# Weights in smaller transfers, masks moved to TensorE and a later order of work in a sparse-attention and feed-forward kernel

## The chip, the cores and the metric

The kernel runs on one core of a Trainium2 chip. The metric is device time in microseconds (us). Before the change it is 330.48 us, the median of three runs (329.52 to 330.79). One execution of each kernel was also profiled; the profile's span is some 2 us shorter than the device time.

The core has five engines that run side by side, each through its own instructions in the order of the program: TensorE (PE in the profile; its weight loads are PEld), VectorE (DVE), ScalarE (ACT), GpSimd (POOL) and SyncE (SP). Here TensorE writes its results to eight banks of the memory called PSUM, which ScalarE and VectorE empty. Loads run on 16 shared DMA engines.

## The reference

```python
scores = scale * np.matmul(q, k.transpose(0, 1, 3, 2))          # 8 batches, 8 heads, 576 positions, 64 wide
mask_local = (rel >= 0) & (rel < 32)                            # heads 0 to 3
mask_strided = (rel >= 0) & (pos[None] % 32 == pos[:, None] % 32)   # heads 4 to 7
attn = softmax(np.where(masks, scores, -1e9)); x = attn @ v
# ... x to (4608 tokens, 512)
h = x @ w_in                       # 512 -> 2048
g = s * np.maximum(h, 0)**2 + b
out = g @ w_out                    # 2048 -> 512
```

## The kernel before

Attention goes batch by batch, in four pairs of heads: Q and K are transposed (TensorE, or a DMA transpose for the strided K of batches 2 to 7), scores go to a PSUM bank, ScalarE takes the exponential, and the product with V follows. The feed-forward runs over nine blocks of 512 tokens: 64 matmuls of 512 columns for `x @ w_in`, ScalarE's relu, VectorE's square, 64 matmuls for `g @ w_out`.

A host-side plan decides the order in which all this is issued. It keeps assumed times: when a load lands, how long an instruction takes. Each engine then gets its instructions in that order. An assumed landing that is wrong makes an engine stand still at the head of its queue, as e1 below shows; the reads wait for their semaphores.

```python
LAT = {"A": 70.0, "V": 70.0, "P": 70.0, "D": 2000.0}      # assumed latency, ns; D is a DMA transpose
...
def load_w_in():
    wv = moe_w_in.rearrange("(c p) f -> p c f", p=128)
    for c, (at, n) in enumerate(((0, 512), (512, 512), (1024, 1024))):
        nc.gpsimd.dma_start(out=w_in_sb[c], in_=wv[:, :, at:at + n])
...
# scores; only batch 0 gets its mask as a matmul (identity times -30000 where masked)
if b == 0:
    nc.tensor.matmul(out=st["s", g][0:nk, c:c + 2 * nq], lhsT=ident[0:nk, 0:nk],
                     rhs=neg_loc if loc else neg_str, start=True, stop=False)
nc.tensor.matmul(out=st["s", g][0:nk, c:c + 2 * nq], lhsT=..., rhs=..., start=b > 0, stop=True)
# the other batches: VectorE multiplies the exponentials by a mask of 0 and 1
nc.vector.tensor_tensor(out=pt[0:nk, 0:2 * n], in0=pt[0:nk, 0:2 * n], in1=mask, op=ALU.mult)
...
by_dma = b >= 2          # strided K, and X of the local pairs, by DMA transpose from batch 2 on
...
def landing(cost):       # assumed landing of the next load in the queue
    nonlocal ring
    ring = max(ring, plan.t + 2000.0) + cost
    return ring
```

While nothing is ready in the first microseconds, the plan issues filler matmuls on a tile of ones (L792 in the profile before) to keep TensorE's clock up.

The softmax here doesn't subtract the row's maximum and nothing guards it: scores larger than these inputs give would overflow.

## Time and profile before

| | before |
|---|---|
| device time, median of 3 | 330.48 us |
| span of the profiled execution | 328.9 us |
| TensorE busy | 319.1 us, 97% |
| VectorE, ScalarE busy | 201.4, 168.8 us |
| granted TensorE clock, mean (1 is full speed) | 0.992 |

A busy time counts a matmul from its start to its modelled end, and matmuls overlap (those of 512 columns last some 380 ns and start 216 ns apart). So this document works with starts. The **needed** time of TensorE is the number of matmuls of each shape by the usual distance from start to next start; the **lost** time is what the actual distances have beyond it (a wait, or half clock, at which 512 columns take 427 ns); the **filler** time is that of the filler matmuls. First start, needed, lost and filler add up to the end of the last matmul by their definition: before, 1.07 + 303.8 + 10.5 + 9.4 = 324.8 us, and the trace has 324.74. All three are worked out from TensorE's timeline; the prediction shows the distances.

### The profile page before, as it was taken

How to read it: one execution, taken by the hardware profiler on the slowest of the kernel's cores; microseconds unless marked ns; L12 is line 12 of the kernel's file. 1: busy time of each engine (PE TensorE's matmuls, PEld its weight loads, DVE VectorE, ACT ScalarE, POOL GpSimd, SP SyncE). 2: the span in 40 equal slices, each digit the busy share in tenths (PEclk: the TensorE clock that was granted, in tenths of full speed). 3: DMA queues.
4: the chain of work that ended last, by engine and by line, in shares of the span. 5: the costliest groups of instructions: out<-in, count | busy, mean ns of one | idle time of the engine just before them, and what ended most of it. 6: DMA issues, size and time to landing. Idle time of an engine off the chain costs nothing.

```text
span 328.9 us, 6347 instructions
## 1 busy us (share of the span) xinstructions
PE 319.1 (97%) x2407; PEld 182.0 (55%) x2407; DVE 201.4 (61%) x553; ACT 168.8 (51%) x319; POOL 82.2 (25%) x112
## 2 busy tenths in 40 slices
PE   8969999999999999999999999999999999999994
PEld 3755655666556666556656556655444544444442
DVE  5665866689877867876777878786332432333211
ACT  2755954499727987754664445553532433233100
POOL 7361549746126434412710000000000000000000
PEclk9998999999999999999999999999999999999999
DMA  8999999999999999949994320111001000100021
GB/s 119 172 177 205 214 154 171 210 170 158 137 146 147 135 58 182 134 64 101 148 117 55 81 84 2 51 52 64 2 32 64 32 34 33 64 31 35 32 98 64
DMA packets 74472, 33.13 MB, mean 101 GB/s; under 512 B 55882, under 2 KB 68810, under 8 KB 74442
## 3 DMA queue, kind: packets, MB, share of 16 engines
q0 software_dynamic: 49984, 18.65, 55.0%
q1 hardware_dynamic: 24458, 14.07, 21.1%
q8 instruction: 19, 0.31, 0.4%
q14 instruction: 11, 0.09, 0.1%
HBM read 38.15 MB, written 9.44 MB: 145 GB/s over the span
## 4 chain that ended last, share of the span: by engine, by line
PE 89%; DMA 6%; DVE 2%; ACT 1%; issue 1%; SPq 0%; POOL 0%; POOLq 0%; DVEq 0%
PE ps_f L601 38%; PE ps_f L566 36%; PE ps_s L421 4%; PE ps_a L473 4%; PE ps_t L350 3%; DMA w_in_sb<-in_moe_w_in_dram 3%; DMA w_out_sb<-in_v_dram 2%; PE ps_t L521 2%; DMA ql<-in_q_dram 1%; PE ps_a L624 1%; PE ps_s L566 1%; ACT u L584 1%; ACT qD_loc L280 1%; DVE qD_str L280 1%; PE ps_f L473 0%
## 5 line engine op out<-in xcount | busy, mean ns | idle before, releaser
L566 PE MATMUL ps_f<-xT,w_in_sb 128*128 128x512 f16 x568 | 154.0, 381 | 0.0
L601 PE MATMUL ps_f<-w_out_sb,gT 128*128 128x512 f16 x576 | 151.8, 379 | 0.4 <-DVE gT L590 0.4
L584 ACT ACTIVATE u<-ps_f 128x512 f16<-128x512 f32 x138 | 82.0, 597 | 83.3 <-PE ps_f L566 61.1
L590 DVE TENSOR_TENSOR gT<-u 128x512 f16<-128x512 f16 x144 | 59.4, 420 | 55.3 <-ACT u L584 54.6
L566 PEld LDWEIGHTS <-w_in_sb 128*128 128x128 f16 x576 | 61.7, 114 | 43.9 <-DMA w_in_sb<-in_moe_w_in_dram 2.1
L601 PEld LDWEIGHTS <-gT 128*128 128x128 f16 x576 | 54.2, 98 | 50.4 <-DVE gT L590 1.1
L435 ACT ACTIVATE pt<-ps_s 128x384 f16<-128x384 f32 (+2 forms) x96 | 44.8, 488 | 15.7 <-PE ps_s L421 15.1
L473 PEld LDWEIGHTS <-pt 72*72 72x72 f16 (+1 forms) x448 | 35.2, 119 | 13.2 <-DVE x_nat L499 0.2
L612 DVE SCALAR_TENSOR_TENSOR o<-ps_f,s_sb,bcs 128x512 f32<-128x512 f32 x36 | 26.8, 745 | 20.6 <-PE ps_f L601 20.3
L499 DVE TENSOR_TENSOR x_nat<-ps_a,rec 72x256 f16<-72x256 f32 (+1 forms) x76 | 35.0, 461 | 1.7
L488 DVE RECIPROCAL rec<-ps_a 72x4 f32<-72x4 f32 (+1 forms) x76 | 13.7, 181 | 18.5 <-PE ps_a L473 16.3
L258 POOL DMA_DIRECT2D v_loc<-in_v_dram x28 | 24.3, 875 | 1.7 <-issue 0.9
L263 POOL DMA_DIRECT2D v_str<-in_v_dram x16 | 13.5, 844 | 44.5 <-PE ps_a L473 22.8
L473 PE MATMUL ps_a<-v_str,pt 72*72 72x65 f16 x204 | 20.9, 196 | 0.0
L421 PE MATMUL ps_s<-qD_str,kTs 128*72 128x144 f16 x128 | 20.1, 226 | 0.2 <-ACT kTs L280 0.2
L280 ACT COPY xT<-ps_t 128x576 f16<-128x576 f16 x16 | 10.2, 637 | 14.1 <-PE ps_t L521 14.0
L421 PEld LDWEIGHTS <-kTs 128*72 128x72 f16 x128 | 13.0, 113 | 5.7 <-ACT kTs L280 0.4
L473 PE MATMUL ps_a<-v_loc,pt 128*96 128x65 f16 x150 | 16.2, 203 | 0.0
L421 PE MATMUL ps_s<-qD_loc,kT_loc 128*128 128x192 f16 x96 | 16.0, 246 | 0.0
L443 DVE TENSOR_TENSOR pt<-pt,mask_str 72x432 f16<-72x432 f16 (+1 forms) x42 | 14.3, 349 | 2.8 <-ACT pt L435 2.5
L443 DVE TENSOR_TENSOR pt<-pt,mask_loc 128x384 f16<-128x384 f16 x42 | 14.2, 351 | 2.2 <-ACT pt L435 1.8
L521 PEld LDWEIGHTS <-x_nat 72*128 72x128 f16 (+1 forms) x152 | 9.9, 102 | 6.5 <-DVE x_nat L499 1.1
(87 smaller groups left out, 253.6 us busy)
## 6 DMA issues: line engine op xcount, KB each, us to landing
out_dram<-o SPq DMA_DIRECT2D x36, 256.0 KB, 2.0
ql<-in_q_dram POOLq DMA_DIRECT2D x8, 288.0 KB, 6.6
kl<-in_k_dram POOLq DMA_DIRECT2D x8, 288.0 KB, 7.5
v_loc<-in_v_dram POOLq DMA_DIRECT2D x28, 80.0 KB, 11.4
w_out_sb<-in_moe_w_out_dram POOLq DMA_DIRECT2D x4, 512.0 KB, 12.0
qs<-in_q_dram POOLq DMA_DIRECT2D x6, 288.0 KB, 8.6
ks<-in_k_dram POOLq DMA_DIRECT2D x6, 288.0 KB, 9.5
v_str<-in_v_dram POOLq DMA_DIRECT2D x16, 72.0 KB, 4.6
```

The lines of the kernel that those rows point to most:

```text
L258: nc.gpsimd.dma_start(out=vl[:, h, 1:LT, 0:D], in_=rest[:, h])
L280: {"A": nc.scalar.copy, "V": nc.vector.tensor_copy, "P": nc.gpsimd.tensor_copy}[eng](**kw)
L421: nc.tensor.matmul(out=st["s", g][0:nk, c:c + 2 * nq], lhsT=(st["k"][:, i * nq:i * nq + nk] if loc else st["k"][:, i, 0:SQ]), rhs=st["q"][ ...
L435: nc.scalar.activation(out=pt[0:nk, 0:2 * n].rearrange("k t c -> k (t c)"), in_=st["s", g][0:nk, 0:2 * n * nq], func=AF.Exp, scale=scale)
L443: nc.vector.tensor_tensor(out=pt[0:nk, 0:2 * n], in0=pt[0:nk, 0:2 * n], in1=mask, op=ALU.mult)
L473: nc.tensor.matmul(out=st["a"][0:nq, j % per, :], lhsT=st["pt", g][0:nk, i, :], rhs=vt[0:nk, 2 * mm + e, j, :])
L499: nc.vector.tensor_tensor(out=st["x"][:, j0:j0 + per, 64 * e:64 * e + 64], in0=st["pa", e, j][0:nq, 0:per, 0:D], in1=st["rec", e, j][0:nq, ...
L566: nc.tensor.matmul(out=gts["h", T, ft], lhsT=w_in_sb[min(ft // 4, 2)][:, ct, :].rearrange("p (c x l) -> p c l x", x=128, l=4)[:, max(ft // ...
L584: nc.scalar.activation(out=gts["u", T, ft], in_=gts["h", T, ft], func=AF.Relu)
L590: nc.vector.tensor_tensor(out=gts[T][:, ft, :], in0=u, in1=u, op=ALU.mult)
L601: nc.tensor.matmul(out=gts["o", T, ts], lhsT=gts[T][:, ft, ts * 128:(ts + 1) * 128], rhs=w_out_sb[:, ft, :], start=(ft == 0), stop=(ft == ...
L612: nc.vector.scalar_tensor_tensor(out=o, in0=gts["o", T, ts], scalar=s_sb[:, 0:1], in1=bcs, op0=ALU.mult, op1=ALU.add)
```

## The change

The intent: use w_in's first quarter as its pieces arrive, relieve VectorE by giving the masks of batches 1 and 2 to TensorE, take K of batch 2 off the DMA queue, and place work on later loads later, where it will not be waited for. The core of the diff, cut:

```diff
-    LAT = {"A": 70.0, "V": 70.0, "P": 70.0, "D": 2000.0}
+    LAT = {"A": 70.0, "V": 70.0, "P": 70.0, "D": 5000.0}
...
+            for c in FIRST:                       # FIRST = (2, 0, 1, 3), the order of use
+                nc.gpsimd.dma_start(out=w_in0[c], in_=wv[:, c, 0:512])
+        else:                                     # issued later, after V of batch 0 is cast
+            nc.gpsimd.dma_start(out=w_in_sb[0], in_=wv[:, :, 512:1024])
+            nc.gpsimd.dma_start(out=w_in_sb[1], in_=wv[:, :, 1024:2048])
...
-        by_dma = b >= 2
+        k_by_dma, x_by_dma = b >= 3, b >= 2
...
-                if b == 0:
+                if b < PE_MASK:                   # PE_MASK = 3
...
-        return ring
+        return ring + (6000.0 if plan.t > 60000.0 else 0.0)
...
     def fetch_qk(b):
+        for mm in range(2):                       # wait until K of the batch before has landed
+            if (b - 1, "kTs", mm) in loaded:
+                nc.gpsimd.tensor_copy(out=gate[0:1, 2 + mm:3 + mm],
+                                      in_=loaded[b - 1, "kTs", mm][0:1, 0, 0:1])
```

Four parts, then: **four transfers** (with the later issue of the weights after them), **masks**, **K of batch 2**, and **placing**.

More of the change, by code (lines that the diff above doesn't have):

```diff
@@ L129 @@
     PS = 512
+    FIRST = (2, 0, 1, 3)
     NFT = DFF // 128
@@ L170 @@
     b_sb = const.tile([128, 1], FP32)
-    w_in_sb = [const.tile([128, 4, n], FP16, name=f"w_in_sb{i}")
-               for i, n in enumerate((512, 512, 1024))]
+    w_in0 = [const.tile([128, 512], FP16, name=f"w_in0{i}") for i in range(4)]
+    w_in_sb = [const.tile([128, 4, n], FP16, name=f"w_in_sb{i}") for i, n in ((1, 512), (2, 1024))]
     w_out_sb = const.tile([128, NFT, DM], FP16)
@@ L265, in load_vs, with load_w_in @@
                 in_=v[b, 4 + h].rearrange("(p j) d -> p j d", j=ST))
-    def load_w_in():
+    def load_w_in(first):
         wv = moe_w_in.rearrange("(c p) f -> p c f", p=128)
-        for c, (at, n) in enumerate(((0, 512), (512, 512), (1024, 1024))):
-            nc.gpsimd.dma_start(out=w_in_sb[c], in_=wv[:, :, at:at + n])
+        if first:
+            for c in FIRST:
[3 more added lines that the diff above has]
+            nc.gpsimd.dma_start(out=w_in_sb[1], in_=wv[:, :, 1024:2048])
     def load_w_out(chunks):
@@ L310 @@
     TB, SB, AB, F1B, F2B = 1, 2, 1, 2, 2
+    PE_MASK = 3
     ps = {tag: [psum.tile([128, PS], FP32, name=f"ps_{tag}{i}") for i in range(n)]
@@ L392, in k_dma @@
             nc.sync.dma_start_transpose(out=st["k"], in_=ks[b % 2][:, 1024 * mm:1024 * mm + 1024])
-        if by_dma and not loc:
+            loaded[b, "kTs", mm] = st["k"]
+        if k_by_dma and not loc:
             plan.post([("in", "ks", b, mm), ("s", (b - 1, m), 2)], {"D": 1000.0}, k_dma,
@@ L398, in pair_steps @@
         for name in ("q", "k"):
-            if by_dma and not loc and name == "k":
+            if k_by_dma and not loc and name == "k":
                 continue
@@ L422, in f @@
                     out=st["s", g][0:nk, c:c + 2 * nq], lhsT=(st["k"][:, i * nq:i * nq + nk] if loc else st["k"][:, i, 0:SQ]),
-                    rhs=st["q"][:, i].rearrange("d e c -> d (e c)"), start=b > 0, stop=True)
-            s = Step(f, (2 if b == 0 else 1) * (2 * nq / 2.4 + 8), needs=[("q", id_), ("k", id_)],
+                    rhs=st["q"][:, i].rearrange("d e c -> d (e c)"), start=b >= PE_MASK, stop=True)
+            s = Step(f, (2 if b < PE_MASK else 1) * (2 * nq / 2.4 + 8), needs=[("q", id_), ("k", id_)],
                      group=group if i % per_s == 0 else None)
@@ L448, in score @@
                             [("p", id_, g)])]
-                if b == 0:
+                if b < PE_MASK:
                     s.posts = [([key], {"A": 170 + 0.83 * 2 * n * nq}, ex, [("p", id_, g), group])]
@@ L545, in x_dma @@
                 in_=st["x"].rearrange("p t d -> p (t d)"))
-        if by_dma and loc:
+        if x_by_dma and loc:
             plan.post([("x", id_, e, nt - 1) for e in range(2)], {"D": 1000.0}, x_dma,
@@ L566, in f @@
             nc.tensor.matmul(
-                out=gts["h", T, ft], lhsT=w_in_sb[min(ft // 4, 2)][:, ct, :].rearrange(
+                out=gts["h", T, ft], lhsT=(w_in_sb[min(ft // 4, 2) - 1][:, ct, :] if ft > 3 else w_in0[ct]).rearrange(
                     "p (c x l) -> p c l x", x=128, l=4)[:, max(ft // 4 - 2, 0), ft % 4],
@@ L572, in ff1 @@
                  for c in ((ct,) if early else range(4))]
-        needs.append(("w_in", ft // 4))
+        needs.append(("w_in", ft // 4) if ft > 3 else ("w_in0", ct))
         if ft == 0 and ct == cts[0] and T >= 2:
@@ L702, in weights_in, with more_weights @@
         nc.gpsimd.tensor_copy(out=gate[0:64, 2:4].bitcast(FP32), in_=vl_stage[64:128, 0, 0, 0:1])
-        load_w_in()
-        ring = 17700.0
-        for keys, cost in ([0], 2900), ([1], 2900), ([2, 3], 5000):
+        load_w_in(True)
+        ring = 18000.0
+        for c in FIRST:
+            arrive([("w_in0", c)], landing(650))
+    def more_weights(eng):
+        load_w_in(False)
+        for keys, cost in ([1], 2800), ([2, 3], 5700):
             arrive([("w_in", c) for c in keys], landing(cost))
     plan.done[("first",)] = 13700.0
-    plan.post([("first",)], {"P": 3500.0}, weights_in, [("w",)])
+    plan.post([("first",)], {"P": 2800.0}, weights_in, [("w1",)])
+    plan.post([("w1",)] + both("vl", 0), {"P": 1500.0}, more_weights, [("w",)])
     plan.done["raw", "v", True, 0] = 16200.0
@@ L747 @@
                     [("fetch_v", b + 1) if b else ("free",)] +
-                    [("k", (b, mk)) for mk in range(4)], {"P": 0.0},
+                    [("k", (bk, mk)) for bk in (b, b + 1 if b > 1 else b) for mk in range(2, 4)],
+                    {"P": 0.0},
                     lambda eng: fetch_qk(b + 2), [("fetch", b + 2)]))
@@ L758 @@
             gr = [Group(*x) for x in (("s", SB), ("s", SB), ("f1", F1B), ("f1", F1B))]
-            cts = (2, 0, 1, 3)
+            cts = FIRST
             f1 += [ff1(T, ft, ct, gr[ft], cts, True) for ct in cts for ft in range(4)]
```

## The prediction

> **What bounds the kernel now.** I read the page first, then the busy time by stretch of 10 us, then TensorE's timeline from 6 to 46 us with GpSimd's beside it, then the list of waits.
>
> ```profile
> PE 319.1 (97%) x2407; PEld 182.0 (55%) x2407; DVE 201.4 (61%) x553; ACT 168.8 (51%) x319; POOL 82.2 (25%) x112
> PE 89%; DMA 6%; DVE 2%; ACT 1%; issue 1%; SPq 0%; POOL 0%; POOLq 0%; DVEq 0%
> ```
>
> And of the groups with every shape kept apart (busy us, mean ns of one | idle before):
>
> ```profile
> L418 PE MATMUL ps_s<-neg_str,ident 72*72 72x144 f16 x16 | 2.7, 227 | 0.1
> L418 PE MATMUL ps_s<-neg_loc,ident 128*128 128x192 f16 x12 | 2.5, 245 | 0.0
> L443 DVE TENSOR_TENSOR pt<-pt,mask_loc 128x384 f16<-128x384 f16 x42 | 14.2, 351 | 2.2 <-ACT pt L435 1.8
> ```
>
> TensorE is the bound: 97% busy, and 89% of the chain that ended last. So time falls only if TensorE is given less work or waits less. The mean durations (227 ns) are latencies; what a matmul costs is the distance from its start to the next start. From the timeline: 512 columns 216 ns (24 of them in 5.34 us), a local score or mask (192 columns) 82 ns, a strided one (144 columns) 63 to 65 ns, a transpose 42 ns (96 columns) or 32 ns (72), a product with V 34 ns. With the counts of the groups: 1168 x 0.216 = 252.3; scores 96 x 0.082 + 128 x 0.063 = 15.9; masks of batch 0 12 x 0.082 + 16 x 0.065 = 2.0; transposes of Q and K 192 x 0.042 + 160 x 0.032 = 13.2; products with V 448 x 0.034 = 15.2; transposes of X 128 x 0.032 + 24 x 0.043 = 5.1. Together 303.7 us of needed work. Of the span of 328.9, 6.9 go before the first useful matmul and 4.2 after the last one, so some 14 are lost between, to waits, to half clock and to the filler matmuls of L792. Adding up, from the timeline, what each start-to-start distance has over the usual one gives where: about 5 before 20 us (3.5 of it filler while the first inputs land), 4.4 from 20 to 30, 0.9 from 30 to 40, 2.9 from 40 to 110, 1.6 from 110 to 230, nothing after.
>
> ```profile
> 10.00:20.00 10.00, 9.58 (x160) 8.23 (x158) 7.53 (x25) 7.96 (x21) 6.50 (x12) 1.00 1.04 165
> 20.00:30.00 10.00, 7.48 (x51) 4.05 (x49) 4.02 (x12) 3.24 (x10) 2.04 (x4) 0.83 1.16 197
> 30.00:40.00 10.00, 9.46 (x94) 5.97 (x93) 8.71 (x23) 8.82 (x17) 5.71 (x8) 1.00 1.15 213
> 40.00:50.00 10.00, 10.00 (x67) 5.49 (x64) 6.10 (x19) 5.52 (x12) 4.14 (x6) 1.00 1.48 162
> ```
>
> The columns are PE, PEld, DVE, ACT and POOL busy, granted clock, DMA share, GB/s. The one bad stretch is 20 to 30: PE 7.48 and a clock of 0.83. The timeline says why:
>
> ```profile
> 22.19 0.62 PE L566 MATMUL ps_s<-xT,w_in_sb 128*128 128x512 f16 x2 [1.95 <-DMA w_in_sb<-in_moe_w_in_dram]
> ...
> 23.87 0.66 PE L521 MATMUL ps_t<-ident,x_nat 96*128 96x96 f16 x6 [0.57 <-DVE x_nat L499]
> ...
> 24.75 1.06 PE L566 MATMUL ps_s<-xT,w_in_sb 128*128 128x512 f16 x2
> ...
> 28.24 5.34 PE L566 MATMUL ps_f<-xT,w_in_sb 128*128 128x512 f16 x24
> ```
>
> The first quarter of w_in comes late, and the matmuls just after the wait run 427 ns apart, at half clock.
>
> ```profile
> 25.92 0.56 POOL L276 DMA_DIRECT2D w_out_sb<-in_moe_w_out_dram  x1 [2.94 <-DMA w_in_sb<-in_moe_w_in_dram]
> 30.84 0.55 POOL L276 DMA_DIRECT2D w_out_sb<-in_moe_w_out_dram  x1 [4.36 <-DMA w_in_sb<-in_moe_w_in_dram]
> ```
>
> Those two issues wait for a free semaphore, so they date the landings of the second quarter (25.4) and of the second half (30.3). The first quarter lands at 22.1, 8.5 us after its issue at 13.6.
>
> **What the Trainium skill says.** "TensorE: Matmul & The Clock Gate", Back-to-back issue gap, gives N/2.4 + 2.5 ns, 216 ns for 512 columns; the trace has 216. For 192 columns it gives 82.5, the trace 82. Part 1 of that page has the clock at half rate after an idle window of about 3.4 us; here 1.95 us of waiting and 0.57 soon after sufficed for some 3 us at half clock, so the trace is harsher. "DMA: Bandwidth & Descriptors", Why a DMA increments its semaphore by 16 and not by 1, says that a transfer runs on up to 16 engines that finish independently and counts as landed with the last. The trace agrees: of the 1,024 packets of 1 KB of the first two quarters, only about 6 per half microsecond are still running from 22.5 to 25, where there were 90 before. A single late engine sets the landing, and 8 of its packets of some 83 ns, a quarter of a transfer, take 0.66 us.
>
> **The change part by part.**
>
> *Four transfers for the first quarter of w_in.* The late engine ends its 32 packets at 22.1 and needs 32 x 0.083 = 2.7 us for them, so it starts at about 19.4. Cut in four, the pieces should land at about 20.1, 20.8, 21.5 and 22.1, in the order in which they are used. TensorE is there at 20.24: the wait of 1.95 goes, and with it the half clock (five matmuls at 0.21 over, 1.05) and most of the 0.57. That is 3.4 us at TensorE. But the next weights limit it. The second quarter is still there at 25.4 and the second half at 30.3, as the same bytes are ahead of them (the later issue, after the casts of V, costs nothing while the queue is full). At 30.3 the kernel before has done 9 or 10 of the 16 matmuls of the second quarter; a TensorE that is not late could have done all 16, 6.5 x 0.216 = 1.4 us, and no more. So of 3.4 us I count 1.4 by 30 us, and up to 0.5 of the 0.9 from 30 to 40.
>
> *Masks of batches 1 and 2 by TensorE.* Added per batch: 12 x 0.082 + 16 x 0.065 = 2.0 us of TensorE, 4.0 in both, all on the bounding engine. Removed: per batch 6 local multiplications of 351 ns, 4 strided ones of 376 and 2 of 295, 4.2 us of VectorE, 8.4 in both; VectorE is not the bound, so this pays only by shorter chains from score to P.
>
> *Transposes of K of batch 2 back on TensorE.* 16 x 0.032 = 0.5 us more TensorE, 1 to 1.3 us of evacuation, and two DMA transposes fewer, which took about 10 us from issue to landing in a full queue. Batch 2's strided scores are ready some 10 us sooner.
>
> *Later placing.* No work; with the assumed landing 3 us later for transposes and 6 us later for loads after 60 us, instructions stand later in TensorE's fixed order. It can remove stalls such as those at 65.4 (0.56), 83.7 (0.2) and 89.5 (0.53): I count 1.6 of the 2.9 us from 40 to 110, helped by the other two parts, and 0.4 of the 1.6 later. The GpSimd waits for landed K delay loads only from batch 3 on, where TensorE has a backlog.
>
> *Sum.* Added 4.0 + 0.5 = 4.5. Removed 1.4 + 0.5 + 1.6 + 0.4 = 3.9, and perhaps 1 to 2 more if the late engine is less late. Near zero. Since the three parts look tuned together I lean to the better half: **329.3 us** against 330.48.
>
> **Rivals.** *The whole early wait is gained*: the 3.4 us of the first wait stay gained, because the second half lands sooner than 30.3 or the masks of batch 1 fill the hole before it (they can't: K of batch 1 lands after 31 us). Then 4.4 + 0.9 + 2 + 0.4 - 4.5, about 3 us gained, 327. For it: the 15 prompt engines are 3 us ahead. Against: the same bytes lie in the same queue. *The masks are simply a cost*: TensorE is 10.00 of 10 busy from 40 on, VectorE's relief shortens nothing that TensorE waits for, and the gain at 20 us turns into waits for the second quarter and the second half: +4.5 - 1.4, about 333.5. For it: the list of waits has only 0.6, 0.4 and 0.3 us of TensorE waiting for VectorE or ScalarE. *Misplacing*: an order made for landings that come later, or earlier, blocks TensorE at its head for several us and drops the clock: 336 or more. The kernel before shows such a wait once, at 20 us.
>
> **Range and chances.** All that is lost from 16 us to 230 us is about 10.5 us; against 4.5 us added, even the loss of none of it gives 6.0, under 2% (6.6). Faster by 2% is thus almost excluded, slower by 2% needs new waits of over 2 us on top of the added work with nothing gained. Range 326.3 to 332.5; chances 0.02, 0.95, 0.03.
>
> **What would show it.** The wait at L566 near 20 us gone or under 0.5, granted clock in 20 to 30 above 0.95; new waits of TensorE for w_in_sb near 25 and 29 to 30, 1 to 2.5 us together; groups of L418-type masks x48 strided and x36 local; VectorE's L443 groups down by 24; VectorE's busy sum about 8 us lower; useful starts from 40 to 110 with under 1.5 us lost. I am wrong if the second half lands well before 30, if waits after 110 change by over 1 us, or if TensorE waits for K or V in batches 2 and 3.

## The result

The changed kernel takes **332.70 us** (332.63 to 332.88, six runs), beside 330.73 us before (329.52 to 331.71, six runs). The ratio is 1.0062, with a 95% interval of 1.0043 to 1.0082. It is slower by 0.6%, within 2%, and just outside the predicted range of 326.3 to 332.5.

The page of the changed kernel, the same two lines, busy times and the chain that ended last:

```profile
PE 322.2 (97%) x2480; PEld 185.0 (56%) x2480; DVE 193.4 (58%) x529; ACT 170.4 (52%) x321; POOL 85.6 (26%) x123
PE 87%; DMA 7%; POOL 2%; ACT 2%; issue 1%; DVE 0%; SPq 0%; POOLq 0%; ACTq 0%
```

TensorE is still the bound, now with 73 matmuls more (one of them a filler). VectorE fell by 8.0 us and nothing came of it. The groups of the changed kernel with shapes kept apart (busy us, mean ns, idle before):

```profile
L451 DVE TENSOR_TENSOR pt<-pt,mask_loc 128x384 f16<-128x384 f16 x30 | 10.3, 348 | 1.1 <-ACT pt L443 0.9
L426 PE MATMUL ps_s<-neg_str,ident 72*72 72x144 f16 x48 | 7.8, 227 | 0.1
L426 PE MATMUL ps_s<-neg_loc,ident 128*128 128x192 f16 x36 | 7.3, 246 | 0.0
```

There are 24 local and 32 strided mask matmuls more, as counted. Busy time by stretch of the changed kernel (columns as in the prediction: PE, PEld, DVE, ACT, POOL, clock, DMA share, GB/s):

```profile
20.00:30.00 10.00, 8.55 (x56) 4.52 (x53) 5.60 (x17) 5.61 (x13) 3.86 (x8) 1.00 1.15 198
30.00:40.00 10.00, 9.29 (x108) 6.47 (x106) 6.97 (x16) 8.78 (x17) 5.62 (x8) 1.00 1.15 212
```

From 20 to 30 us PE rose from 7.48 to 8.55 and the clock from 0.83 to 1.00: the early wait is gone. TensorE's timeline shows what came in its place:

```profile
18.87 0.68 PE L574 MATMUL ps_s<-xT,w_in 128*128 128x512 f16 x2
...
25.02 3.62 PE L574 MATMUL ps_f<-xT,w_in_sb 128*128 128x512 f16 x16
29.39 2.13 PE L574 MATMUL ps_f<-xT,w_in_sb 128*128 128x512 f16 x9 [0.75 <-DMA w_in_sb<-in_moe_w_in_dram]
```

The first matmul on w_in starts at 18.87 in place of 22.19 without a wait; the second quarter's 16 run from 25.02; then TensorE waits for the second half of w_in until 29.39. The account of the two profiled executions, in us of TensorE:

| | needed | lost 16 to 40 | lost 40 to 110 | lost after 110 | lost in all | filler | last matmul ends |
|---|---|---|---|---|---|---|---|
| before | 303.8 | 5.9 | 2.6 | 1.2 | 10.5 | 9.4 | 324.7 |
| changed | 308.3 | 4.0 | 1.9 | 1.6 | 8.3 | 9.1 | 326.8 |

Needed rose by 4.56, lost fell by 2.22 and filler by 0.29: 2.05 together, which is how much later the last matmul ends. The tail after it is 0.36 shorter, so the span grew by 1.7.

### The profile page after: what moved, and what is told of

The parts are those of the page before. It is cut to its first block, busy times and chain, and to the rows that moved or that the text cites. A ratio compares the mean times of both kernels' runs of the same rounds, so it can differ in the third digit from the quotient of the medians.

```text
span 330.6 us, 6484 instructions
## 1 busy us (share of the span) xinstructions
PE 322.2 (97%) x2480; PEld 185.0 (56%) x2480; DVE 193.4 (58%) x529; ACT 170.4 (52%) x321; POOL 85.6 (26%) x123
## 4 chain that ended last, share of the span: by engine, by line
PE 87%; DMA 7%; POOL 2%; ACT 2%; issue 1%; DVE 0%; SPq 0%; POOLq 0%; ACTq 0%
PE ps_f L609 37%; PE ps_f L574 35%; DMA ql<-in_q_dram 5%; PE ps_s L429 4%; PE ps_a L481 4%; PE ps_t L357 3%; DMA w_out_sb<-in_v_dram 2%; PE ps_t L529 1%; PE ps_s L426 1%; PE ps_a L632 1%; ACT qD_loc L286 1%; POOL w_in L273 1%; POOL v_loc L286 1%; PE ps_f L481 0%; ACT kT_loc L286 0%
## 5 line engine op out<-in xcount | busy, mean ns | idle before, releaser
L609 PE MATMUL ps_f<-w_out_sb,gT 128*128 128x512 f16 x576 | 148.7, 379 | 0.0
L574 PE MATMUL ps_f<-xT,w_in_sb 128*128 128x512 f16 x432 | 116.0, 379 | 0.8 <-DMA w_in_sb<-in_moe_w_in_dram 0.8
L574 PEld LDWEIGHTS <-w_in_sb 128*128 128x128 f16 x432 | 46.1, 113 | 34.8 <-DMA w_in_sb<-in_moe_w_in_dram 1.2
L481 PEld LDWEIGHTS <-pt 72*72 72x72 f16 (+1 forms) x448 | 29.3, 120 | 10.8
L574 PE MATMUL ps_f<-xT,w_in 128*128 128x512 f16 x136 | 35.2, 379 | 0.1
L574 PEld LDWEIGHTS <-w_in 128*128 128x128 f16 x144 | 15.3, 114 | 11.0
L429 PE MATMUL ps_s<-qD_str,kTs 128*72 128x144 f16 x128 | 16.3, 226 | 0.2 <-ACT kTs L286 0.2
L481 PE MATMUL ps_a<-v_str,pt 72*72 72x65 f16 x204 | 15.5, 197 | 0.0
L286 ACT COPY qD_loc<-ps_t 64x576 f16<-64x576 f16 x16 | 10.1, 633 | 3.7 <-PE ps_t L357 3.6
L664 POOL COPY gate<-kTs 1x1 f16<-1x1 f16 x8 | 2.0, 251 | 37.6 <-DMA kTs<-ks 37.6
```

Source lines behind the costliest of these rows:

```text
L286: {"A": nc.scalar.copy, "V": nc.vector.tensor_copy, "P": nc.gpsimd.tensor_copy}[eng](**kw)
L429: nc.tensor.matmul(out=st["s", g][0:nk, c:c + 2 * nq], lhsT=(st["k"][:, i * nq:i * nq + nk] if loc else st["k"][:, i, 0:SQ]), rhs=st["q"][ ...
L481: nc.tensor.matmul(out=st["a"][0:nq, j % per, :], lhsT=st["pt", g][0:nk, i, :], rhs=vt[0:nk, 2 * mm + e, j, :])
L574: nc.tensor.matmul(out=gts["h", T, ft], lhsT=(w_in_sb[min(ft // 4, 2) - 1][:, ct, :] if ft > 3 else w_in0[ct]).rearrange("p (c x l) -> p c ...
L609: nc.tensor.matmul(out=gts["o", T, ts], lhsT=gts[T][:, ft, ts * 128:(ts + 1) * 128], rhs=w_out_sb[:, ft, :], start=(ft == 0), stop=(ft == ...
```

## The experiments

Sixteen kernels ran. Kernels of one call ran on one chip, beside runs of the kernel before on it; those spread from 328.3 to 333.1 us in the fast state, so runs of different calls are compared by their ratios to before. The record marks every result correct, that of e17 too, although e17 leaves out the masks of two batches: so this check does not tell whether a mask is applied.

| run | transfers | masks of batches | K of batch 2 | placing | median us | ratio (95%) | needed | lost 16-40, 40-110 |
|---|---|---|---|---|---|---|---|---|
| e1 | four | 0 | DMA | before | 334.09 | 1.0122 (1.0072-1.0172) | 303.8 | 4.5, 7.4 |
| e2 | four | 0 | TensorE | later | 329.12 | 0.9980 (0.9933-1.0026) | 304.3 | 5.6, 2.5 |
| e3 | four | 0 | DMA | later | 330.46 | 1.0010 (0.9957-1.0062) | 303.8 | 4.3, 3.5 |
| e4 | one | 0-2 | DMA | before | 336.18 | 1.0172 (1.0122-1.0222) | 307.8 | 5.1, 6.4 |
| e5 (changed) | four | 0-2 | TensorE | later | 333.03 | 1.0080 (1.0050-1.0110) | 308.3 | 3.7, 1.9 |
| e6 | four | 0-1 | TensorE | later | 331.76 | 1.0050 (1.0009-1.0090) | 306.3 | 3.9, 3.4 |
| e7 | four | 0-7 | TensorE | later | 342.32 | 1.0362 (1.0332-1.0392) | 318.4 | 3.9, 2.0 |
| e8 | four | 0-2 | TensorE | before | 331.95 | 1.0053 (1.0023-1.0083) | 308.3 | 3.5, 1.8 |
| e9 | four | 0 | TensorE | before | 329.38 | 0.9970 (0.9934-1.0006) | 304.3 | 4.9, 2.1 |
| e10 | one | 0 | TensorE | before | 329.35 | 0.9965 (0.9930-1.0001) | 304.3 | 4.7, 2.9 |
| e11 | one | 0 | DMA | later | 330.24 | 1.0000 (0.9959-1.0042) | 303.8 | 3.8, 2.5 |
| e12 | four | 0-2 | DMA | before | 333.69 | 1.0089 (1.0041-1.0137) | 307.8 | 3.6, 1.9 |
| e15 | four | 0, 1-2 twice | TensorE | later | 336.10 | 1.0179 (1.0141-1.0218) | 312.4 | 3.9, 1.4 |
| e17 | four | 0, 1-2 none | TensorE | later | 330.53 | 1.0002 (0.9967-1.0037) | 304.3 | 4.6, 3.3 |
| e16 | four, and the second half in two | 0 | TensorE | before | 328.89 | 0.9957 (0.9923-0.9991) | 304.3 | 3.9, 2.3 |

(e13 is the kernel before, one look, told below.) The edits were these, each against the changed kernel or, where said, together:

```diff
# masks of n batches (e2: 1, e6: 2, e7: 8)
-    PE_MASK = 3
+    PE_MASK = n
# K of batch 2 by DMA transpose
-        k_by_dma, x_by_dma = b >= 3, b >= 2
+        k_by_dma, x_by_dma = b >= 2, b >= 2
# placing as before
-    ... "D": 5000.0}
+    ... "D": 2000.0}
-        return ring + (6000.0 if plan.t > 60000.0 else 0.0)
+        return ring
-        for mm in range(2): if (b - 1, "kTs", mm) in loaded: nc.gpsimd.tensor_copy(out=gate...)   # and its condition
# one transfer: w_in0 is one tile again, and all of w_in is issued at once with before's assumed landings
```

**What the parts do alone.** e1 keeps the four transfers only.

> The kernel before with the four transfers of w_in's first quarter alone (masks of batches 1 and 2 on VectorE, K of batch 2 by DMA, placing as before). Theory A, TensorE's account (time changes by the TensorE work added less the TensorE time no longer lost): no work is added, 303.8 us needed as before; the wait near 20 us and its half clock go, a wait of about 1 us for the second half of w_in comes near 28 us: 1.5 to 2.5 us faster than before, ratio 0.993 to 0.995, some 328.6 us. Theory B, the gain was given back later (a later stage sets the end, or the next weights cap it): within 0.5 us of before, ratio 0.999 to 1.001.

It was 1.2% slower than before, against both theories. From 16 to 40 us it lost 4.5 in place of 5.9, as hoped, but from 40 to 110 us 7.4 in place of 2.6. TensorE's and ScalarE's timeline of e1 says where:

```profile
82.52 1.14 ACT L286 COPY v_str<-vs 72x512 f16<-72x512 f16 x2 [2.50 <-DMA vs<-in_v_dram]
82.52 0.50 DVE L286 COPY v_str<-vs 72x512 f16<-72x512 f16 x2 [1.69 <-DMA vs<-in_v_dram]
...
84.58 0.81 PE L574 MATMUL ps_f<-xT,w_in_sb 128*128 128x512 f16 x3 [2.39 <-ACT u L592]
...
85.91 1.05 PE L609 MATMUL ps_f<-w_out_sb,gT 128*128 128x512 f16 x2
```

ScalarE and VectorE stand at a cast of V whose load has not landed; the relu behind it in ScalarE's order comes late; TensorE waits 2.39 us for the PSUM bank that the relu empties; and from 85.91, 1.3 us after the wait has ended, matmuls run at half clock (2 in 1.05 us).

> The changed kernel, but only batch 0's masks by TensorE, batches 1 and 2 masked by VectorE again. Theory A: 24 local and 32 strided mask matmuls fewer, 24 x 0.082 + 32 x 0.065 = 4.05 us less TensorE work, so 4.05 us faster than the changed kernel: about 328.7 us, ratio to before 0.994. Rival C, VectorE's relief buys shorter chains: TensorE's lost time between 30 and 110 us rises by 2 us or more, and the kernel is at 330.7 or above, ratio 1.000 or more.

e2 is 0.998 of before, 0.8 to 1.0% better than the changed kernel's 1.0062 and 1.0080: about 3 us for 4.05 us of work. Its profiled execution waited 1.6 us for the second half of w_in, the longest such wait of all.

> The changed kernel with the masks of batches 1 and 2 on VectorE and K of batch 2 by DMA transpose, so: the four transfers and the later placing alone. Theory A: 4.05 + 0.51 = 4.56 us less TensorE work than the changed kernel, about 328.1 us, ratio to before 0.992. If K of batch 2 on TensorE was what kept TensorE supplied from 60 to 75 us, lost time there rises by over 0.5 us and this run is no faster than the one that only takes the masks back.

e3, on the same chip as e1, differs from it by the placing alone: 330.46 against 334.09. So with K of batch 2 on DMA the placing does take away e1's stall. But e3 is no faster than e2, although it has 0.5 us less to do.

> The kernel before with only the masks of three batches and K of batch 2 on TensorE (w_in as before, placing as before). Theory A: 4.56 us more TensorE work, the lost time of 20 to 40 us as before: about 335.2 us, ratio 1.014. Rival C: VectorE's relief and the early K take away 1.5 us or more of the lost time: 333.7 or less, ratio 1.009 or less.

This kernel was not what its text says: K of batch 2 was left on DMA by mistake, so it shows the masks alone, 4.05 us of work. It was 1.7% slower, more than that work explains, with a stall of the same kind as e1's:

```profile
88.81 0.83 ACT L285 COPY kp<-kl 96x768 f16<-96x768 f16 x1 [3.88 <-DMA kl<-in_k_dram]
88.88 0.36 DVE L285 COPY kp<-kl 96x768 f16<-96x768 f16 x1 [2.79 <-DMA kl<-in_k_dram]
...
90.18 0.59 PE L573 MATMUL ps_f<-xT,w_in_sb 128*128 128x512 f16 x2 [2.75 <-ACT u L591]
```

**The changed kernel with more or fewer masks, and without the placing.**

> The changed kernel as it is, once more beside the others on one chip. Both theories: 332.7 us within 0.3, ratio about 1.006; lost TensorE time about 8.3 us of which under 1 us from 66 to 110.

> The changed kernel with masks of batches 0 and 1 by TensorE, batch 2 by VectorE. Theory A (TensorE's account): 12 x 0.082 + 16 x 0.065 = 2.0 us less TensorE work than the changed kernel; if the lost time stays the same, 2.0 faster, 330.7. With half of what e2 showed coming back as lost time (10.2 + 9.6 filler against 8.3 + 9.1, 2.3 in all), 0.9 faster: 331.8. Rival C (batch 2's masks are the ones that pay, as lost time from 66 to 110 fell from 1.7 to 0.8 with them): no faster than the changed kernel.

> The changed kernel with the masks of all eight batches by TensorE: 60 more local and 80 more strided mask matmuls, 60 x 0.082 + 80 x 0.065 = 10.1 us. Theory A: TensorE has no spare time after 110 us (1.5 us lost there in all), so between 8.6 and 10.1 us slower than the changed kernel, 341.3 to 342.8, ratio 1.032 to 1.037. Rival C (VectorE's relief, 10.5 us more off it, shortens what TensorE waits for): under 7 us slower, 339.7 or less.

e5 repeats the result. One batch of masks fewer (e6) gains 1.3 us by the medians for 2.0 us of work, within what theory A allowed. Five batches more (e7) cost 9.3 us for 10.1 us of work, although VectorE was relieved of them. Rival C, that VectorE's relief pays, falls with e7: its lost time is 8.1, the changed kernel's 8.0 in e5.

> The changed kernel with the assumed landings of before (2 us for DMA transposes, no 6 us on loads after 60 us, no waits of GpSimd for landed K): the four transfers, the masks and K of batch 2 on TensorE stay. Theory D, formed from e1 and e4: ScalarE and VectorE take their instructions in order, and casts of q, k and v placed for a load that has not landed block the relu and the squares behind them, so TensorE waits for a PSUM bank and drops to half clock. Expects waits of ScalarE or VectorE for DMA of over 2 us between 60 and 110, TensorE losing 4 us or more there against 0.8, time 335.5 to 338. Rival: the placing is worth nothing by itself, the stalls of e1 and e4 came from batch 2's K by DMA; then within 1 us of the changed kernel.

e8 was 1.1 us faster than e5 on the same chip, and its profile has no wait over 0.6 us after 20 us. Theory D, that the placing is what prevents the stall in the changed kernel, is wrong. With K of batch 2 on TensorE the placing gains nothing; whether it costs 1 us is not settled, since the intervals overlap, and of the 1.25 us by which the last matmul of e5's trace ends later, 0.76 are filler.

**K of batch 2.**

> The four transfers and K of batch 2 on TensorE; masks of batches 1 and 2 on VectorE, placing as before. Theory E, formed from e1, e3, e4 and e8: the stalls of 2.4 and 2.8 us at 82 and 87 us in e1 and e4 come from batch 2's K going by DMA transpose in an order that differs from before's; K on TensorE takes them away, and the later placing is not needed. Expects no wait of TensorE over 1 us after 40, lost 8 to 9.5 us in all, 304.3 us needed, so 2.0 to 3.5 us faster than e8: 328.5 to 330. Theory D (the placing is what prevents the stalls): a wait of 2 us or more between 60 and 110 and a time above 332.

> The kernel before with K of batch 2 on TensorE alone. Theory E: 0.5 us more TensorE work, lost time from 66 to 110 falls from 1.6 to about 1: between 0.5 faster and 0.5 slower than before, ratio 0.998 to 1.002. If the order as such is brittle (any change of it brings a stall), ratio 1.008 or more with a wait over 1.5 us between 60 and 110.

> The kernel before with the later placing alone (K of batch 2 by DMA, w_in as before). Theory D: the waits of ScalarE and VectorE for loads after 60 us vanish and so up to 1 us of TensorE's lost time: ratio 0.996 to 1.000. Theory E: the placing as such costs up to 1 us, as e8 against e5: ratio 1.000 to 1.004.

> The changed kernel without the placing and with K of batch 2 by DMA: differs from e8 only in K. Theory E: the stall returns, TensorE waits 2 us or more at one place between 75 and 95 us and drops to half clock, lost time there 4 us or more against 0.8 in e8, time 334.5 to 337. Otherwise (masks on TensorE already cure it): within 1 us of e8, 331 to 333.

e9 is e1 with K of batch 2 on TensorE, and it goes from 1.0122 to 0.9970. Its timeline has the same casts of V with no wait ahead of them:

```profile
80.60 1.14 ACT L286 COPY v_str<-vs 72x512 f16<-72x512 f16 x2
81.43 0.49 DVE L286 COPY v_str<-vs 72x512 f16<-72x512 f16 x2
```

By the landings in the two traces, V, Q and K of those loads come at 77.2, 80.9 and 83.8 us in e9 and at 82.5, 84.6 and 88.9 in e1, from issues within 1.4 us of each other. e9 has two DMA transposes less in the queue; that these are why the loads land sooner is likely, and not shown, since the order of the other transfers changed too. (The two ran on different chips; both ratios are to before on the same one.) e10, K alone, is 0.9965, with an interval that just reaches 1. Theory E's reason for a gain there was not seen: lost time from 66 to 110 is 1.6 in e10's trace as in before's, and in the two traces of before the only cast after 60 us that waits for its load waits 0.7 us (e13). All four pairs that differ in K alone do point the same way: e10 and before, e9 and e1, e2 and e3 (0.998, 1.001), e8 and e12 (1.0053, 1.0089). e9 and e10, on one chip, differ by the four transfers alone, and they are equal. e11, the placing alone, is 1.000, which both theories allowed.

e12 differs from e8 by K alone. It was slower, 1.0089 against 1.0053 (on different chips, and the intervals overlap), and its runs spread from 331.6 to 336.1 where e8's lie within 331.7 and 332.9. But its profiled execution was one of the fastest, at 331.94, and shows no stall, so the stall that theory E expected there was not seen; whether the slower executions had it, no trace shows.

**The early wait, and what a mask costs.** The kernel before once more:

> The kernel before, one more look. If the wait of 1.95 us for the first quarter of w_in is the kernel's, it shows again within 0.5 us, with half clock after it and 4 us or more lost from 20 to 30. If it was that execution's late landing, the quarter lands 5.3 to 7.5 us after its issue in place of 8.5, the wait is under 1.2 us, and 1.7 to 3 us are lost from 20 to 30, with a wait of about 1 us for the second half of w_in near 28 us in its place.

```profile
20.91 0.62 PE L566 MATMUL ps_s<-xT,w_in_sb 128*128 128x512 f16 x2 [1.14 <-DMA w_in_sb<-in_moe_w_in_dram]
...
22.60 0.66 PE L521 MATMUL ps_t<-ident,x_nat 96*128 96x96 f16 x6 [0.57 <-DVE x_nat L499]
...
23.48 1.06 PE L566 MATMUL ps_s<-xT,w_in_sb 128*128 128x512 f16 x2
```

The wait is there, but 1.14 us in place of 1.95, as the second branch expected; half clock still follows, and 2.3 us are lost from 20 to 30 (1.9 more from 16 to 20, where the wait now begins). The wait for the second half that this branch expected did not come. The landing decides. The tile view gives the time from issue to landing of the first quarter in one transfer, in the profiled executions of e4 and e10:

```profile
DMA to landing us min/median/max: 7.5/7.5/7.5
```

```profile
DMA to landing us min/median/max: 5.3/5.3/5.3
```

It is 8.5 before, 7.5 in e4, 5.3 in e10, and by the traces 7.1 in e13 and 6.5 in e11. In e10 and e11 TensorE waited 0.1 us for it at most. In four transfers the first piece lands 3.5 to 4.1 us after its issue in every run, and the last 6.0 to 6.8 after the first one's issue. So what the four transfers may buy is a guard against a late landing. No time shows it (e9 and e10 are equal), and the split is not the only candidate: the same edit also issues the second quarter later (at 18.0 us in place of 14.4), and no run has one without the other.

> The changed kernel with each mask matmul of batches 1 and 2 issued twice, in the same order on every engine: 24 x 0.082 + 32 x 0.065 = 4.05 us more TensorE work, nothing taken from VectorE. If mask matmuls cost their full spacing: 3.6 to 4.1 us slower than the changed kernel, about 336.5, ratio 1.018 to 1.020. If TensorE has slack under them (they fill waits of batch 1 near 35 to 42 us): 2 to 3 us slower, ratio 1.012 to 1.016.

> The changed kernel without any mask in batches 1 and 2, in the same order on every engine (wrong result on purpose): VectorE keeps its relief and TensorE loses the 4.05 us. If the masks' whole cost is TensorE time: 3.6 to 4.1 faster than the changed kernel, about 328.8, ratio 0.995; and faster than e2 (329.1, ratio 0.998), where VectorE does the masks, by VectorE's relief, about 1 us. If the relief is worth nothing: equal to e2.

```diff
# e15: beside the mask matmul
+                if 0 < b < PE_MASK:
+                    nc.tensor.matmul(out=..., lhsT=ident[0:nk, 0:nk], rhs=neg_loc if loc else neg_str, start=False, stop=False)
# e17: the plan is left as it is
-                if b < PE_MASK:
+                if b == 0:
-    ... start=b >= PE_MASK, stop=True)
+    ... start=b > 0, stop=True)
```

e17, the changed kernel and e15 have the same order on every engine and the same work on VectorE; they differ in 0, 4.05 and 8.1 us of mask matmuls. The ratios are 1.0002, 1.0062 and 1.0080, and 1.0179. By 330.1 us, the first dose costs 2.0 to 2.6 us and the second 3.3 to 3.9; both together, on one chip, 5.8 us for 8.1 of work. (Each ratio is uncertain by some 0.35%, 1.2 us, so that the doses differ is not shown by the times alone.) The lost time agrees: 10.3, then 8.0 to 8.3, then 7.7. Of the first dose some 2 us fill places where TensorE would have waited anyway. Two such waits of e17, in TensorE's timeline:

```profile
36.34 0.50 PE L429 MATMUL ps_s<-qD_loc,kT_loc 128*128 128x192 f16 x4 [0.25 <-ACT kT_loc L286]
...
66.01 0.41 PE L357 MATMUL ps_t<-ident,qp 96*128 96x96 f16 x6 [0.40 <-ACT xT L286]
```

In the changed kernel the second one is gone and the first is 0.16:

```profile
35.46 0.26 PE L429 MATMUL ps_s<-qD_loc,kT_loc 128*128 128x192 f16 x1 [0.16 <-ACT kT_loc L286]
```

And e17, with masks on no engine, is no faster than e2 (0.998), where VectorE has them: the relief of VectorE is worth nothing that these runs can see.

> e9 (four transfers, K of batch 2 on TensorE, masks of batches 1 and 2 on VectorE, placing of before) with the second half of w_in in two transfers of 512 columns in place of one of 1024. The third quarter should land about 2.5 us before the fourth, near 27 us, so that the wait of TensorE for w_in_sb near 29 us (0.9 in e9) goes: 0.5 to 1.2 us faster than e9, ratio to before 0.993 to 0.996. If the freed time turns into waits for Q and K of batch 1 (lands after 31 us): within 0.3 of e9, ratio 0.996 to 0.998.

```diff
# on e9
-            nc.gpsimd.dma_start(out=w_in_sb[1], in_=wv[:, :, 1024:2048])
+            for c in (1, 2):
+                nc.gpsimd.dma_start(out=w_in_sb[c], in_=wv[:, :, 512 + 512 * c:1024 + 512 * c])
```

```profile
24.91 5.56 PE L575 MATMUL ps_f<-xT,w_in_sb 128*128 128x512 f16 x25
30.93 0.43 PE L358 MATMUL ps_t<-ident,qp 96*128 96x96 f16 x6 [0.47 <-ACT qp L287]
```

The 25 matmuls on the second and third quarter now run on end, where the changed kernel stopped after 16; the next wait is for Q of batch 1. e16 takes 328.89 us, ratio 0.9957 (0.9923 to 0.9991): faster than before by 0.4%, and its interval lies wholly below the changed kernel's. It beats both. Against e9 the gain is 0.1% with overlapping intervals, so the split itself is not proved by time, only by the wait that went.

## Why the prediction was wrong

The range missed by 0.2 us, and the sign of the difference was wrong. By its steps:

- **What bounds the kernel** was right: e15 and e7 show that more work on TensorE lengthens the time. Three readings were off. The matmuls just after the wait of 1.95 us ran at full clock; half clock came 1.7 us later, after the second wait, as the clock (the column after POOL's) shows:

```profile
22.00:23.00 1.00, 0.81 (x11) 0.61 (x11) 0.01 (x1) 0.00 (x0) 0.56 (x1) 1.00 1.21 209
24.00:25.00 1.00, 1.00 (x8) 0.63 (x7) 0.57 (x2) 0.11 (x1) 0.00 (x0) 0.50 1.13 212
```

  The 10.5 us "from 16 us to 230" are the loss of the whole span; from 16 us on it is 9.7. And the 2.9 and 1.6 lost from 40 to 110 and later are 2.6 and 1.2 by the account above.
- **Added work, 4.0 + 0.5**, was right: 4.56.
- **Four transfers, 1.4 + 0.5 from 16 to 40 us**, was right for the two traces: 1.9, and the rest turned into the predicted wait for the second half, at 29.4. But the step took one execution for the kernel. It expected the pieces at 20.1 to 22.1 us, by the lag of the late engine in that one execution; they landed at 17.7 to 20.3, and the transfer in one piece landed between 5.3 and 8.5 us after its issue. Against e10, where it was early, four transfers gain nothing (e9, 0.9970 against 0.9965).
- **Later placing, 1.6 from 40 to 110 and 0.4 after**, is the step that failed. In place of 2.0 us removed, the traces have 0.8 from 40 to 110 and 0.4 more lost after it. The stalls that I hoped to see removed at 83.7 and 89.5 went, and the longest wait left after 40 us is 0.35, but small ones stayed, and e8 has the same 1.8 us lost there without the placing. So the 0.8 is not the placing's. It goes with the masks: the traces with masks of three or more batches have 1.4 to 2.0 there (e4 with its stall apart), those with fewer 2.1 or more. e12 has 1.9 with the masks but neither the placing nor K of batch 2 on TensorE; e17, the changed kernel without the masks of two batches, has 3.3. A wait that a mask fills only makes the mask cheaper; it does not make the kernel faster.
- **K of batch 2** I had put down as a cost of 0.5 us with a vague benefit. Alone it gives 0.35% (e10), more than it costs if that is real, since the interval just reaches 1. The cause stays open: e10's trace lost as much from 66 to 110 as before's. Where a cast of ScalarE or VectorE did stand at a late load (e1), K on TensorE went with loads 3.7 to 5.3 us sooner and no such stall (e9).
- **The sum.** The working came to 0.6 us slower, 331.1; I then moved to 329.3, "since the three parts look tuned together". No view of the profile said so. The working alone, with a range of the same width, would have held the result. With the terms as measured the two traces give 4.56 more work, 2.22 less lost and 0.29 less filler, 2.05 us later.
- **The signs.** The wait gone, the clock, the mask counts and VectorE's 8 us came as written. The new wait for w_in was 0.75 us in place of 1 to 2.5, and 1.9 us were lost from 40 to 110 in place of under 1.5.
- **The rivals.** "The masks are simply a cost" gave 333.5 and was the nearest. Its reason was right too, TensorE waits little for VectorE, but the cost is not 4.05: 2.0 to 3.3 us (e17 and the changed kernel; e9 and e8, 0.9970 and 1.0053; e2 and the changed kernel), as the masks fill waits for ScalarE. "Misplacing" did not happen in the changed kernel, but it did in e1 and e4, at 1.2 and 1.7%.

So the 0.6 to 0.8% of the changed kernel is: masks about +0.8%, K of batch 2 about -0.35%, four transfers 0, placing between 0 and +0.3%. That the parts add is an estimate: with K by DMA they do not (e1 is 1.0122, e11 is 1.000, both together, e3, are 1.001; and masks added to e1, which is e12, give 1.0089). All but the masks' part lie within the noise of these runs.

## What to carry to other kernels

In these runs work moved to the engine that sets the time was paid there, less the waits that it happened to fill, and relief of an engine that TensorE seldom waited for paid nothing that could be seen. Before you price a wait for a DMA, look at a second execution: here the landing moved by 1.4 us between two executions of the same kernel. In a kernel of fixed order, a cast whose load is late blocks everything behind it on its engine (e1), so shortening the DMA queue is worth a trial beside guessing the landings better. And write down the sum that the working gives.

## What the Trainium skill lacked or had wrong

- "TensorE: Matmul & The Clock Gate", Back-to-back issue gap, says that in a real stream of weight loads and matmuls 512 columns sustain about 131 ns each and that N/2.4 + 2.5 over-counts. Here they run 216 ns apart wherever TensorE neither waits nor is at half clock (24 in 5.34 us, each with its own weight load); the formula fits and the 131 is not seen.
- The same page, Part 1, gives an idle window of about 3.4 us before the clock halves, and tells of a kernel with frequent short idles, without their length. Here waits of 1.95 and 0.57, of 1.14 and 0.57 (e13), of 2.39 (e1) and of 2.75 us (e4) were each followed by matmuls some 427 ns apart, which began 0.6 to 1.7 us after the longest wait had ended. Waits of 1.64 (e2) and 1.19 us (e10) for w_in were followed by none. What decides is not shown.
- The same page, Part 4: PE-mode transpose, puts a transpose of 128x128 at about 275 ns in a kernel. For the smaller ones here the trace has durations of 197 (72 columns) and 206 ns (96) at the median. What one costs in a stream is the distance, 32 and 42 ns; the formula of the first point gives 32.5 and 42.5, but the section does not say that it holds for transposes.
- "DMA: Bandwidth & Descriptors", Why a DMA increments its semaphore by 16 and not by 1, says that the last of 16 engines decides the landing, but no page says how far the landing of one transfer moves between executions: the first quarter of w_in, 512 KB, took 5.3 to 8.5 us from issue to landing in five profiles.
